# Casts, squares and folds at other steps of a fused cross-covariance attention and StarReLU kernel

## The chip, the cores and the metric

The kernel runs on one core of a Trainium2 chip. A core has a matrix engine (TensorE, in the profile PE, with its weight loads as PEld), a vector engine (VectorE, DVE), an activation engine (ScalarE, ACT), a general engine (GpSimd, POOL), and SyncE (SP), which here only issues DMAs. Each engine works through its own queue of instructions, and they wait for each other by semaphores. The metric is the device time of one execution in microseconds, lower is better; 718.1 us is the median of five runs before the change (718.03 to 718.57).

## The reference

Two layers are chained. The first is a cross-covariance attention over channels, for 4 batches of 6080 rows and 256 channels:

```python
qn = q / (np.linalg.norm(q, axis=1, keepdims=True) + 1e-06)
kn = k / (np.linalg.norm(k, axis=1, keepdims=True) + 1e-06)
s = kn.transpose(0, 2, 1) @ qn / tau
a = softmax(s)                       # over the last axis
x = (v @ a).reshape(24320, 256)
```

The second is a feed-forward layer with 2048 hidden units:

```python
h = x @ w_in
r = np.maximum(h, 0.0)
g = s * (r * r) + b                  # s and b are single numbers
out = g @ w_out
```

## The kernel before, in words

**Folding.** The attention matrix `a` of a batch (256 x 256) is multiplied into `w_in` once (`wa`, 256 x 2048), so that the hidden layer is `h = v @ wa`. The constant `b` enters as one row, `rowconst`, added at the end, and `s` as a factor of the evacuation.

**Groups and steps.** The 24320 rows of v are cut into groups of 512. A group has 16 steps, one for each 128 hidden units (`m`). The main loop runs over `s = 16 g + m`, and in each step `mm1` issues two 512-column matmuls into half of a PSUM tile `h_ps`; there are two such tiles. After every odd step ScalarE's `relu` turns one full `h_ps` tile into fp16 `r`, and so frees it: the tile written in steps 20 and 21 is written again in step 24, which can't start before the relu issued in step 21 has ended. Squares of `r` give `g`: for groups other than the first and the last, the table `SQUARES` says that two of them run on ScalarE (after steps 3 and 5 of the group) and the larger ones on VectorE (after 8 and 12, and after step 0 of the next group).

**The second matmul.** It runs one group late. For most groups the product of `g` with `w_out` is done with seven instead of eight half-size products (`seven_items`), each of 16 small matmuls, issued seven in a step from the fourth step on. They need combined weights (`T1`, `T2`, `T3`, `N4`, made from the pieces of `w_out` by `combine_w` and `cast_w`) and sums of quarters of `g` (`S1` to `S4`, by `sums_of`, VectorE). Three PSUM areas X, Y, Z are used in turn by the seven products X, Z, X, Y, X, Z, X; Z and Y lie in one tile. After each product VectorE evacuates it (`evacuate`: `u` for three of them, `o_sb` for four), and the next product in the same tile waits for that. The first group uses the plain product instead (`plain_mm2`) and needs `w_out` in fp16, piece by piece (`cast_w_out`, four pieces).

**The next batch beside it.** While the groups of batch b - 1 run, the gram matrix and the norms of batch b are made from chunks of 512 rows of k and q (`Gram`). For each chunk `norm_ops` gives up to five operations: the square of k (ScalarE), the square of q (VectorE), a first fold of both (1024 elements), a second fold (512 elements), and an accumulating DMA on GpSimd's queue (`into_first`).

**What sets the order.** Everything on the side is put at a step by hand with `at_step(s, f)`: after the matmuls of step s the functions of that step issue their instructions, in the order in which they were put there, and `po` keeps the program order on each engine. The tuples `CO`, `RC`, `CW`, `CT` hold the steps of the work on `w_out`. For the chunks of a batch, `sc` is the (fractional) step of chunk c; its loads go to `sc - 16`, its gram matmuls from `sc` on, and its norm operations to `int(sc) + 3`, and 3, 6, 9 and 12 steps later. For batch 1 (groups 0 to 10) `sc` is 26 + 6.75 c, for batch 2 it is 182 + 9.75 c, for batch 3 it is 374 + 9.75 c. The raw chunks and the fp32 pieces of `w_out` share one pool of eight buffers (`qk_pool`), so the last reader of a piece decides when a later chunk can be loaded. The squares of the chunks have two buffers (`sq_pool`).

Of the kernel before, what the change touches and what calls it, by code (L numbers as in the profile page):

```python
# [17 lines left out]
def kernel(  # L18
# [15 lines left out]
    B, N, C = q.shape  # L34
# [14 lines left out]
    NG = (NT + TG - 1) // TG  # L49
# [6 lines left out]
    def po(ins):  # L56

        tc.keep_in_program_order(ins)
        return ins
# [29 lines left out]
    T1, T2, T3, N4 = (wpool.tile([P, NP, P], FP16, name=n) for n in ("T1", "T2", "T3", "N4"))  # L89
# [287 lines left out]
    def group(g):  # L377
        t0 = g * TG
        return t0, min(TG, NT - t0) // P
# [3 lines left out]
    def load_v(g):  # L383
        t0, nj = group(g)
        v16 = vpool.tile([P, TG // P, C], FP16, tag="v16", name="v16")
        po(nc.gpsimd.dma_start(  # L386
            out=v16[:, :nj, :],
            in_=v_flat[t0 : t0 + nj * P, :].rearrange("(p j) c -> p j c", j=nj)))
        v_tiles[g] = v16

    def transpose_v(g):
        _, nj = group(g)
        v16 = v_tiles.pop(g)
        vT_ps = ps_o.tile([P, CH, TG], FP16, tag="o_ps", name="vT_ps")
        for j in range(nj):
            for ch in range(CH):
                po(nc.tensor.transpose(vT_ps[:, ch, ts(j, P)], v16[:, j, ts(ch, P)], ident16))
        vT = vtpool.tile([P, CH, TG], FP16, tag="vT", name="vT")
        po(nc.vector.tensor_copy(out=vT[:, :, : nj * P], in_=vT_ps[:, :, : nj * P]))
        vT_tiles[g] = vT  # L400

    def crossbar_v(g):

        _, nj = group(g)
        v16 = v_tiles.pop(g)
        vT = vtpool.tile([P, CH, TG], FP16, tag="vT", name="vT")
        for j in range(nj):
            po(nc.sync.dma_start_transpose(out=vT[:, :, ts(j, P)], in_=v16[:, j, :]))
        vT_tiles[g] = vT
# [126 lines left out]
    def combine_w(i, k):  # L536

        for n in (2 * k, 2 * k + 1):
            for p in (2 * i, 2 * i + 1):
                w = w_pieces[p].rearrange("p (i h) c -> p h i c", h=2)  # L540
                B11, B12 = w[:, 0, :, :P], w[:, 0, :, P:]
                B21, B22 = w[:, 1, :, :P], w[:, 1, :, P:]
                part = ts(p, 2)
                if n == 0:
                    po(nc.vector.tensor_sub(T1[:, part, :], B12, B11))
                elif n == 1:
                    po(nc.vector.tensor_sub(B12, B22, B12))
                elif n == 2:
                    po(nc.vector.tensor_add(B11, B11, B12))
                else:  # L550
                    po(nc.vector.tensor_sub(N4[:, part, :], B21, B11))

    def cast_w_out(i):
        if i == 0:
            po(nc.vector.tensor_copy(out=w_out16[:, ts(i, 4), :], in_=w_pieces[i]))
        else:
            po(nc.scalar.copy(out=w_out16[:, ts(i, 4), :], in_=w_pieces[i]))

    def cast_w(T, i):
        w = w_pieces[i].rearrange("p (i h) c -> p h i c", h=2)  # L560
        po(nc.scalar.copy(out=T[:, ts(i, 2), :], in_=w[:, 0, :, :P] if T is T2 else w[:, 0, :, P:]))
# [4 lines left out]
    def at_step(s, f):  # L566
        side.setdefault(int(s), []).append(f)
# [8 lines left out]
        out=s_out, in0=s_bc, scalar1=1.0 / (LAM * LAM))))  # L576

    RC = (13, 16, 19, 21, 23)
    CO = (7, 14, 18, 24)
    CW = (17, 20, 25, 27)  # L580
    CT = (32, 34, 36, 38)
    for i in range(NPIECE):
        at_step(CO[i], lambda i=i: cast_w_out(i))
    for i in range(NPIECE + 1):
        at_step(RC[i], lambda i=i: rowconst_sum(i))
    at_step(30, rowconst_mm)
    for i in range(NPIECE):
        at_step(CW[i], lambda i=i: combine_w(i // 2, i % 2))
        at_step(CT[i], lambda i=i: cast_w(T2, i))
        at_step(CT[i] + 6, lambda i=i: cast_w(T3, i))  # L590
    for g in range(NG):
        if g >= 3:
            at_step(max(g - 4, 0) * FT + 2, lambda g=g: load_v(g))
        if g >= 1:
            if g == 1:
                at_step(12, lambda g=g: transpose_v(g))
            else:
                at_step((g - 2) * FT + 6, lambda g=g: crossbar_v(g))
    for b in range(1, B):
        gr = grams[b]  # L600
        w0 = first_group[b - 1] * FT + (26 if b == 1 else 6)
        w1 = first_group[b] * FT - 3
        NCH = len(gr.chunks)
        fin_len = 54
        span = (w1 - fin_len) - w0 - 12
        n = NCH * JC
        for c in range(NCH):
            sc = w0 + span * c * JC / n
            at_step(max(3, sc - 16), lambda gr=gr, c=c: gr.load(c))
            if c == 0:  # L610
                at_step(sc, gr.start)
            for j in range(JC):
                at_step(w0 + span * (c * JC + j) / n, lambda gr=gr, c=c, j=j: gr.mm(c, j))

            def norm_step(gr=gr, c=c, sc=sc):
                ops = gr.norm_ops(c)
                for i, f in enumerate(ops):
                    at_step(int(sc) + 2 + 1 + i * 3, f)
            at_step(sc + 1, norm_step)

        def fin_step(gr=gr, s=w1 - fin_len):
            ops = gr.finish_ops()
            for i, f in enumerate(ops):
                at_step(int(s) + 1 + (FIN[i] if i < len(FIN) else FIN[-1] + 3 * (i - len(FIN) + 1)), f)
        at_step(w1 - fin_len - 12, fin_step)
# [15 lines left out]
    def mm1(g, m):  # L641

        _, nj = group(g)
        n = nj * P
        vT = vT_tiles[g]
        i, fh = divmod(m, 2)
        if fh == 0:
            h_tiles[g, i] = h_tile("h_ps")
        h_ps = h_tiles[g, i][:, fh, :]
        for b, p0, p1 in segments(g):  # L650
            wa = grams[b].wa
            for ci in range(CH):
                if p1 - p0 == P:
                    dst, src = h_ps[:, :n], vT[:, ci, :n]
                else:
                    dst = h_ps[:, :n].rearrange("f (j p) -> f j p", p=P)[:, :, p0:p1]
                    src = vT[:, ci, :n].rearrange("f (j p) -> f j p", p=P)[:, :, p0:p1]
                po(nc.tensor.matmul(dst, wa[:, ci, ts(m, P)], src,  # L658
                                    start=(ci == 0), stop=(ci == CH - 1), skip_group_check=True))
        if m == FT - 1:  # L660
            del vT_tiles[g]
# [9 lines left out]
    def square(g, i0, i1, engine):  # L671

        n = group(g)[1] * P
        if i0 == 0:
            g_tiles[g] = gpool.tile([P, 2, NP, TG], FP16, tag="g16", name="g16")
        src = r_tiles[g, i0 // 2][:, :, i0 % 2 : i0 % 2 + i1 - i0, :n]
        dst = g_tiles[g][:, :, i0:i1, :n]
        if engine is nc.scalar:
            po(nc.scalar.activation(out=dst, in_=src, func=AF.Square))  # L679
        else:  # L680
            po(nc.vector.tensor_mul(dst, src, src))  # L681
# [79 lines left out]
    def seven_items(g):  # L761
# [56 lines left out]
        for n, (name, a, w, after) in enumerate(products):  # L818
            for i in range(NP):
# [15 lines left out]
    plain = {0, NG - 1}  # L835
    PLAG = {0: 11, NG - 1: 5}

    SQUARES = {3: (0, 1, nc.scalar), 5: (1, 2, nc.scalar), 8: (2, 4, nc.vector),
               12: (4, 6, nc.vector)}
# [10 lines left out]
    for s in range(NS + FT):  # L850
        g, m = divmod(s, FT)
        if g < NG:
            mm1(g, m)
        for f in early.pop(s, []):
            f()

        if m == SHIFT and 0 < g and g - 1 not in plain:
            items = seven_items(g - 1)
            work.append((items, 8 if g == NG - 1 else 7))
        if work:  # L860
            items, n = work[0]
            for f in items[:n]:
                f()
            del items[:n]
            if not items:
                work.pop(0)
        for gp in plain:
            for mp in range(FT):
                if s == gp * FT + PLAG[gp] + (mp * 4 // 3 if gp == 0 else mp):
                    plain_mm2(gp, mp)  # L870
        if g < NG and m % 2 == 1:
            relu(g, m // 2)
            if g in plain:
                late = g > 0 and m // 2 % 2 == 0
                square(g, m // 2, m // 2 + 1, nc.scalar if late else nc.vector)
        if g < NG and g not in plain and m in SQUARES:
            square(g, *SQUARES[m])
        if g == NG - 1 and m in LAST:
            LAST[m]()
        elif m == 0 and 0 < g and g - 1 not in plain:  # L880
            square(g - 1, 6, 8, nc.vector)
        elif 0 < g and g - 1 not in plain and m in SUMS:
            sums_of(g - 1, SUMS[m])
        for f in side.pop(s, []):
            f()
# [34 lines left out]
```

## Time and profile before

| What | Value |
|---|---|
| median of five runs | 718.1 us |
| the profiled execution | 718.4 us, its span from first to last instruction 716.6 us |
| mean granted TensorE clock | 0.998 |
| TensorE matmul busy | 697.4 us, 97% of the span |
| VectorE busy | 624.2 us, 87% |
| ScalarE busy | 544.7 us, 76% |
| GpSimd busy | 110.8 us, 15% |
| relu on ScalarE (L668) | 384 instructions, 1014 ns mean |
| squares of `r` on VectorE (L681) | 150 instructions, 1165 ns mean |
| squares of `r` on ScalarE (L679) | 97 instructions, 1035 ns mean |

Times are counted from the first instruction of the span. Step 0 starts at 37.4 us, step 16 at 49.8, step 32 at 63.7, step 48 at 78.7. In a row of the timeline the first number is the start, the second the duration, and "xN" says that N equal instructions follow each other in it; "[idle before <-releaser]" names what ended a longer idle time. Since an engine begins its next instruction a little before the last one's end, the time that an instruction takes on its queue is read from one start to the next.

### The profile page before, as it was taken

How to read it: one execution, taken by the hardware profiler on the slowest of the kernel's cores; microseconds unless marked ns; L12 is line 12 of the kernel's file. 1: busy time of each engine (PE TensorE's matmuls, PEld its weight loads, DVE VectorE, ACT ScalarE, POOL GpSimd, SP SyncE). 2: the span in 40 equal slices, each digit the busy share in tenths (PEclk: the TensorE clock that was granted, in tenths of full speed). 3: DMA queues.
4: the chain of work that ended last, by engine and by line, in shares of the span. 5: the costliest groups of instructions: out<-in, count | busy, mean ns of one | idle time of the engine just before them, and what ended most of it. 6: DMA issues, size and time to landing. Idle time of an engine off the chain costs nothing.

```text
span 716.6 us, 17491 instructions
## 1 busy us (share of the span) xinstructions
PE 697.4 (97%) x7421; PEld 503.6 (70%) x7421; DVE 624.2 (87%) x877; ACT 544.7 (76%) x592; POOL 110.8 (15%) x189
## 2 busy tenths in 40 slices
PE   4699999999999999999999999999999999999998
PEld 2456777776677777777677777777668777777777
DVE  4889999988789989998889899998887888888886
ACT  5779877787777777778777778777877777777874
POOL 4532323202101222111010222110000000000000
PEclk9999999999999999999999999999999999999999
DMA  9999999636565978444661887853323333321201
GB/s 234 207 258 172 154 155 159 122 91 124 110 125 109 136 134 144 112 89 93 136 149 53 148 133 126 152 91 75 100 63 75 94 71 75 97 60 46 82 31 75
DMA packets 87454, 83.47 MB, mean 116 GB/s; under 512 B 56304, under 2 KB 62256, under 8 KB 87376
## 3 DMA queue, kind: packets, MB, share of 16 engines
q0 software_dynamic: 26608, 43.40, 38.6%
q1 hardware_dynamic: 60192, 37.64, 21.7%
q8 instruction: 58, 0.95, 0.6%
q10 hardware_dynamic: 576, 1.31, 0.5%
q14 instruction: 20, 0.16, 0.1%
HBM read 78.91 MB, written 24.90 MB: 145 GB/s over the span
## 4 chain that ended last, share of the span: by engine, by line
PE 93%; DMA 3%; DVE 2%; ACT 2%; issue 0%; ACTq 0%; DVEq 0%
PE h_ps L658 45%; PE o_ps L826 40%; PE s_ps L148 4%; PE wa_ps L327 2%; DMA qk<-in_k_dram 1%; DMA raw<-in_q_dram 1%; ACT sq L177 1%; PE o_ps L730 1%; DVE f L191 1%; PE o_ps L704 0%; ACT r L668 0%; ACT r L269 0%; DVE sq L174 0%; PE n_ps L244 0%; DVE o_sb L686 0%
## 5 line engine op out<-in xcount | busy, mean ns | idle before, releaser
L668 ACT ACTIVATE r<-h_ps 128x1024 f16<-128x1024 f32 (+1 forms) x384 | 388.4, 1014 | 151.8 <-PE h_ps L658 148.1
L658 PE MATMUL h_ps<-vT,wa 128*128 128x512 f16 (+7 forms) x1632 | 452.5, 365 | 0.6 <-ACT wa L320 0.5
L826 PEld LDWEIGHTS <-S 128*128 128x128 f16 x2944 | 198.0, 98 | 84.8 <-issue 0.2
L826 PEld LDWEIGHTS <-g 128*128 128x128 f16 x2208 | 155.0, 98 | 74.1
L681 DVE TENSOR_TENSOR g<-r 128x2048 f16<-128x2048 f16 (+2 forms) x150 | 174.8, 1165 | 13.9 <-ACT r L668 13.4
L826 PE MATMUL o_ps<-T,S 128*128 128x128 f16 x2208 | 183.4, 219 | 0.1
L658 PEld LDWEIGHTS <-wa 128*128 128x128 f16 x1632 | 135.9, 98 | 20.6 <-ACT wa L320 0.8
L826 PE MATMUL o_ps<-w_out,g 128*128 128x128 f16 x1472 | 134.3, 219 | 0.2 <-DVE u L686 0.2
L686 DVE SCALAR_TENSOR_TENSOR o_sb<-o_ps,s_out,u 128x256 f32<-128x256 f32 x138 | 66.5, 482 | 50.8 <-PE o_ps L826 48.9
L679 ACT ACTIVATE g<-r 128x1024 f16<-128x1024 f16 (+1 forms) x97 | 100.4, 1035 | 0.2
L148 PE MATMUL s_ps<-qk 128*128 128x256 f16 (+1 forms) x384 | 72.2, 291 | 13.6 <-ACT qk L139 9.3
L386 POOL DMA_DIRECT2D v<-in_v_dram x48 | 31.0, 648 | 263.3 <-DMA vT<-v 196.3
L686 DVE SCALAR_TENSOR_TENSOR u<-o_ps,s_out,rowconst 128x256 f32<-128x256 f32 x138 | 65.9, 478 | 0.0
L826 PE MATMUL o_ps<-w_out,S 128*128 128x128 f16 x736 | 63.5, 219 | 0.0
L826 PE MATMUL o_ps<-N,g 128*128 128x128 f16 x736 | 63.4, 219 | 0.0
L207 POOL DMA_DIRECT2D f<-f x30 | 26.3, 876 | 224.9 <-DVE f L191 180.6
L755 DVE TENSOR_TENSOR S<-S,g 128x2048 f16<-128x2048 f16 (+1 forms) x47 | 56.4, 1201 | 1.3
L177 ACT ACTIVATE sq<-qk 128x1024 f16<-128x1024 f16 (+2 forms) x53 | 54.5, 1041 | 3.9 <-DMA qk<-in_k_dram 2.6
L753 DVE TENSOR_TENSOR S<-g 128x2048 f16<-128x2048 f16 (+1 forms) x47 | 56.1, 1193 | 0.0
L759 DVE TENSOR_TENSOR S<-g,S 128x2048 f16<-128x2048 f16 x46 | 55.9, 1216 | 0.0
L757 DVE TENSOR_TENSOR S<-g 128x2048 f16<-128x2048 f16 x46 | 55.9, 1216 | 0.0
L148 PEld LDWEIGHTS <-qk 128*128 128x128 f16 (+1 forms) x384 | 33.0, 103 | 20.8 <-ACT qk L139 9.8
(83 smaller groups left out, 314.0 us busy)
## 6 DMA issues: line engine op xcount, KB each, us to landing
out_dram<-o_sb SPq DMA_DIRECT2D x42, 512.0 KB, 3.0
v<-in_v_dram POOLq DMA_DIRECT2D x47, 256.0 KB, 4.8
qk<-in_k_dram POOLq DMA_DIRECT2D x42, 256.0 KB, 6.7
qk<-in_q_dram POOLq DMA_DIRECT2D x42, 256.0 KB, 7.7
f<-f POOLq DMA_DIRECT2D x30, 128.0 KB, 3.3
vT<-v SPq DMA_TRANSPOSE x182, 3.0
out_dram<-o_sb SPq DMA_DIRECT2D x10, 256.0 KB, 4.8
w<-in_moe_w_out_dram POOLq DMA_DIRECT2D x4, 512.0 KB, 9.8
```

Of the source, the lines that this page charges most:

```text
L148: po(nc.tensor.matmul(self.s_ps[:, ch, :], qc[:np_, j, ts(ch, P)], kc[:np_, j, :], start=(c == 0 and j == 0 and ch == 0), stop=(c == len(s ...
L177: po(nc.scalar.activation(out=st["sq"][:np_, a, js, :], in_=(qc, kc)[a][:np_, js, :], func=AF.Square))
L658: po(nc.tensor.matmul(dst, wa[:, ci, ts(m, P)], src, start=(ci == 0), stop=(ci == CH - 1), skip_group_check=True))
L668: po(nc.scalar.activation(out=r16[:, :, i % 2, :n], in_=h_tiles.pop((g, i))[:, :, :n], func=AF.Relu))
L679: po(nc.scalar.activation(out=dst, in_=src, func=AF.Square))
L681: po(nc.vector.tensor_mul(dst, src, src))
L686: po(nc.vector.scalar_tensor_tensor(out=dst, in0=src, scalar=s_out, op0=ALU.mult, in1=add, op1=ALU.add))
L753: po(nc.vector.tensor_add(T[1], A21, A22))
L755: po(nc.vector.tensor_sub(T[2], T[1], A11))
L757: po(nc.vector.tensor_sub(T[3], A11, A21))
L759: po(nc.vector.tensor_sub(T[4], A12, T[2]))
L826: po(nc.tensor.matmul(st[name][:, j, :], a()[:, i, ts(j, P)], w[:, i, :], start=first, stop=last, skip_group_check=True))
```

## The change

It moves instructions to other steps; none is added or taken away.

- `w_out`'s casts to fp16 (pieces 1 to 3) go to steps 12, 14 and 18, from 14, 18 and 24. The casts of `T2` go to 28, 28, 31, 32, from 32, 34, 36, 38, and those of `T3` to 34, 36, 38, 40, from 38, 40, 42, 44.
- In group 1 the two ScalarE squares go to steps 5 and 7 of the group, from 3 and 5.
- A table `LATER` shifts single norm operations (0: square of k, 1: square of q, 2 and 3: folds, 4: the accumulating DMA) of chunks 0, 1, 2 and 11 of batch 1, and of chunks 4 and 6 of batches 2 and 3, by that many steps. The operations are put in place three steps ahead of the chunk instead of one after it, so that a negative shift is possible.

```diff
-    CO = (7, 14, 18, 24)
+    CO = (7, 12, 14, 18)
     CW = (17, 20, 25, 27)
-    CT = (32, 34, 36, 38)
+    CT = (28, 28, 31, 32)
+    CT3 = (34, 36, 38, 40)
...
         at_step(CT[i], lambda i=i: cast_w(T2, i))
-        at_step(CT[i] + 6, lambda i=i: cast_w(T3, i))
+        at_step(CT3[i], lambda i=i: cast_w(T3, i))
...
+    LATER = {(1, 0): {2: 3, 3: 1}, (1, 1): {0: 6, 1: 3, 2: 3, 3: 3, 4: 3},
+             (1, 2): {0: 4, 2: 1, 3: 1, 4: 1}, (1, 11): {2: 1, 3: 1}}
+    for b in range(2, B):
+        LATER.update({(b, 4): {2: 1}, (b, 6): {0: -2}})
...
                 ops = gr.norm_ops(c)
+                later = LATER.get((gr.b, c), {})
                 for i, f in enumerate(ops):
-                    at_step(int(sc) + 2 + 1 + i * 3, f)
-            at_step(sc + 1, norm_step)
+                    at_step(int(sc) + 3 + i * 3 + later.get(i, 0), f)
+            at_step(sc - 3, norm_step)
...
-        if g < NG and g not in plain and m in SQUARES:
-            square(g, *SQUARES[m])
+        squares = {**SQUARES, 3: (), 5: SQUARES[3], 7: SQUARES[5]} if g == 1 else SQUARES
+        if g < NG and g not in plain and squares.get(m):
+            square(g, *squares[m])
```

## The prediction

> **What bounds the kernel now.** I began with the page's engine totals and then the busy time of each engine in stretches (columns: stretch, its length, then busy us and number of instructions for TensorE matmul, weight load, VectorE, ScalarE, GpSimd; granted clock, DMA share, GB/s).
>
> ```profile
> PE 697.4 (97%) x7421; PEld 503.6 (70%) x7421; DVE 624.2 (87%) x877; ACT 544.7 (76%) x592; POOL 110.8 (15%) x189
> ...
> 43.00:76.00 33.00, 32.64 (x250) 21.09 (x248) 31.02 (x51) 30.17 (x37) 7.96 (x15) 1.00 1.10 187
> 76.00:136.00 60.00, 60.00 (x643) 44.16 (x642) 57.57 (x85) 47.62 (x51) 17.02 (x26) 1.00 1.11 156
> 242.00:265.00 23.00, 22.99 (x246) 16.68 (x245) 21.36 (x31) 17.96 (x19) 4.46 (x7) 1.00 0.99 158
> ```
>
> TensorE's busy share says it never stops after 76 us, but its spans are modelled and overlap. So I read its timeline by start times instead: a 512-column matmul is followed after 0.216 us, a 256-column one after 0.109, a 128-column one after 0.056. What exceeds these is lost. From 43 us on, the losses over 0.06 us are few. Four places, each a row and the next:
>
> ```profile
> 55.45 0.60 PE L730 MATMUL o_ps<-w_out,g 128*128 128x256 f16 x4
> 56.10 0.59 PE L658 MATMUL h_ps<-vT,wa 128*128 128x512 f16 x2
> ...
> 69.61 0.80 PE L826 MATMUL o_ps<-T,S 128*128 128x128 f16 x7
> 70.25 0.38 PE L148 MATMUL s_ps<-qk 128*128 128x256 f16 x2
> ...
> 71.72 0.61 PE L826 MATMUL o_ps<-T,S 128*128 128x128 f16 x6
> 72.55 0.22 PE L826 MATMUL o_ps<-w_out,g 128*128 128x128 f16 x1 [0.21 <-DVE u L686]
> ...
> 262.50 0.22 PE L826 MATMUL o_ps<-w_out,g 128*128 128x128 f16 x1
> 262.73 0.59 PE L658 MATMUL h_ps<-vT,wa 128*128 128x512 f16 x2
> ```
>
> Row by row: 4 x 0.109 after 55.45 is 55.89, the next starts at 56.10 (0.22 lost); 7 x 0.056 after 69.61 is 70.00, next 70.25 (0.25); 6 x 0.056 after 71.72 is 72.06, next 72.55 (0.12 + 0.38); 262.56 against 262.73 (0.18). The whole list: 0.04 at 50.0; 0.22, 0.12 and 0.13 at 55.8, 57.7 and 59.6; 0.25, 0.12, 0.38 and 0.05 at 69.8, 71.8, 72.1 and 72.7; 0.07 at 139.5; 0.12 and 0.18 at 247.6 and 262.5; the same two at 420.3 and 435.2; and, away from the change, 0.17 at 43.1 and 0.14 at 703.5. TensorE is the bound, and **1.96 us** is all that lies in the change's reach.
>
> Who is late shows in the other queues at those times. ScalarE ahead of 56.10:
>
> ```profile
> 54.08 1.06 ACT L679 ACTIVATE g<-r 128x1024 f16<-128x1024 f16 x1
> 55.03 1.02 ACT L668 ACTIVATE r<-h_ps 128x1024 f16<-128x1024 f32 x1
> 55.93 1.07 ACT L679 ACTIVATE g<-r 128x1024 f16<-128x1024 f16 x1
> 56.88 1.03 ACT L668 ACTIVATE r<-h_ps 128x1024 f16<-128x1024 f32 x1
> 57.78 1.06 ACT L557 CAST w_out<-w 128x1024 f16<-128x1024 f32 x1
> ```
>
> The relu at 55.03 (its input ready at 54.31) frees the `h_ps` buffer that step 24 writes; it ends at 56.05, and step 24 starts at 56.10. Squares (L679) and a cast (L557) stand ahead of three relus in turn. VectorE ahead of 70.04 and 72.55:
>
> ```profile
> 68.95 0.69 DVE L191 TENSOR_TENSOR f<-sq 128x1024 f16<-128x1024 f16 x1
> 69.55 0.48 DVE L686 SCALAR_TENSOR_TENSOR u<-o_ps,s_out,rowconst 128x256 f32<-128x256 f32 x1
> 69.95 1.22 DVE L757 TENSOR_TENSOR S<-g 128x2048 f16<-128x2048 f16 x1
> 71.08 0.42 DVE L191 TENSOR_TENSOR f<-f 128x512 f16<-128x512 f16 x1
> 71.42 0.69 DVE L174 TENSOR_TENSOR sq<-qk 128x1024 f16<-128x1024 f16 x1
> 72.02 0.48 DVE L686 SCALAR_TENSOR_TENSOR u<-o_ps,s_out,rowconst 128x256 f32<-128x256 f32 x1
> ```
>
> Each evacuation `u` ends where the third and the fourth product can start (70.03, 72.50); folds and a square of the next batch stand just ahead of it.
>
> **What the Trainium skill says.** "TensorE: Matmul & The Clock Gate", section "Wait — 56ns, not 53.3ns?", gives back-to-back warm matmuls as 55.6 and 215.7 ns for 128 and 512 columns; the trace's 56 and 216 agree, so the sums above measure loss. The same page, on engine queue depths, has ScalarE and VectorE as strict FIFO: what is moved ahead delays all behind it, as the rows above show. "Perfetto Trace Analysis", section "Identifying the Most-Contended Engine", calls matmul busy share a bad measure; here 60.00 of 60 agrees. "VectorE: DVE Perf Modes", section "The perf-mode tier table", has a 2048-element 16-bit tensor_tensor at 1224 ns; the trace has 1.22.
>
> **The change part by part.** No instruction is added or removed; TensorE's and SyncE's orders stay as they are. On one queue an instruction costs its start-to-start time: relu 0.92, ScalarE square or large cast 0.95, small cast 0.30; VectorE 2048-element ops 1.13, square or first fold 0.60, second fold 0.34, evacuation 0.40.
>
> *Casts and squares, steps 7 to 31.* The casts of pieces 1 to 3 move to steps 12, 14, 18. Step 12's fills idle ScalarE time: free at 47.03, done at 48.07, next relu at 48.24. Its data landed at 45.16. It also ends the 0.04 at 50.0. The others take the slots of the earlier two; their data landed at 46.67 and 48.07, before 49.16 and 52.23. Group 1's squares move from steps 19 and 21 to 21 and 23. So the relu of step 21 starts at 54.31 and ends at 55.33; square; relu of step 23 at 56.18 to 57.21; square; relu of step 25 waits for that square's end (58.16; it reuses the tile) and runs 58.19 to 59.24. TensorE asks for these at 55.84, 57.58 and 59.31 (56.10, 57.96 and 59.82 less the losses up to there). All are in time, the last by 0.02 after a release of 0.05. Gain 0.04 + 0.47. The T2 casts at 28 and 31 come after their inputs (the last combine for them ends at 61.2) and end by 64.4; the 0.12 at 71.8, a wait for T2's last piece, goes. T3's last cast ends near 71.4 instead of 76.5; its product starts later.
>
> *Folds and squares of batch 1, chunks 0 to 2.* VectorE is one unbroken queue here. It starts group 1's square (57.94, waiting for a relu) at 57.77. Adding start-to-start times, with the own-result waits seen before, S1 starts at 66.28, S2 at 67.54, then `u` at once: 68.67 to 69.15, where TensorE asks at 69.33 (69.84 less 0.51; later ones likewise). Then S3 (69.07), fold (70.20), second `u` 70.80 to 71.28, asked at 71.29. On to the evacuation of the fifth product at 77.55 to 78.02, asked at 78.09, now behind a fold and a square of chunks 1 and 2. The relu freeing step 42's buffer, now without two squares and casts ahead of it, ends at 71.13, asked at 71.6. The pinch: between 57.77 and 82 VectorE idled 0.17 (before 57.94), 0.44 (72.42 to 72.86) and 0.60 (78.99 to 79.59), 1.21 in all, and the same work stands in it after the change. So it can come out **1.21** earlier, not the 1.30 that TensorE's list (0.04 + 0.47 + 0.79) offers; 0.09 returns as a wait for the next `u`, near 84.6.
>
> *Chunk 11 of batch 1.* A fold (0.60) goes behind an evacuation: the 0.07 at 139.5 goes. *Batches 2 and 3, chunk 4.* The fold goes behind the second `u`: 0.12 each. *Chunk 6.* A ScalarE square moves from behind step 243's square into step 241, where ScalarE idled 0.84 ahead of step 243's relu; 0.95 of work delays that relu some 0.05, and the relu that TensorE waits for at 262.7 comes about 0.9 earlier: 0.18 each. Together 0.07 + 0.59. Its data landed at 238.3, 18 us ahead.
>
> *GpSimd.* One accumulating DMA moves from step 47 to 50, behind a load of v and of chunk 6; it no longer holds them (they were issued at 78.99 behind its 78.38). Buffers freed earlier by T3 let chunk 4's load go at about 66 instead of 67.3. Nothing on TensorE waited for a DMA after 43 us. I take nothing; chunk 2 still lands about 3 us ahead of its use.
>
> Sum: 1.21 + 0.07 + 0.59 = 1.87. The three slacks below 0.1 may leak; I take 0.02 for it. The profiled execution took 718.4 (span 716.6, 1.8 around it), 0.3 over the median of 718.1; the change alters only the span, to 714.75. From the median: **716.25**.
>
> **The rivals.** A measurement of this kernel tells 0.2%, 1.44 us, from no change.
>
> *The slacks fail.* The relu of step 25, the second `u` and the fifth evacuation have 0.02, 0 and 0.07 in hand. If each is late by 0.2, the first part keeps 0.6 to 0.7: 716.8 (down to 717.3 if later batches also give half). For: VectorE has no idle left. Against: every duration is measured and the order of work fixed.
>
> *No effect.* The stalls are as long elsewhere, or the engines' waits just move by one instruction: 718. For: VectorE 57.57 of 60 after 76 us. Against: the list of idle times above.
>
> *Slower.* The fold of chunk 1 at step 44 stands ahead of the square of step 44 and the fifth evacuation, and waits for a ScalarE square that stands behind step 41's relu. If that ended after 76.3 the whole VectorE queue would stop, and TensorE with it, one for one. It should end at 73.3; to eat 1.87 and cost 1.44 more it must come 6.3 late: 719.6. Against: no ScalarE backlog over 1 us exists there.
>
> **How the numbers follow.** As forecast 0.73 (716.0 to 716.6); slacks fail 0.17; no effect 0.07; slower 0.03. The first is faster by over 0.2%, with a fifth of the second: 0.76; within 0.2%: 0.20; slower: 0.04. The range 715.8 to 717.2 holds the first and most of the second; its low end is all 1.96 and a little scatter.
>
> **What would show it.** No L658 row of TensorE more than 0.1 late at 55 to 60; the relu of step 21 near 54.3; `u` before the first fold, near 68.7; VectorE unbroken from 57.8 to 80; step 50's S1 near 80.9; no loss at about 247 and 262. Wrong if a new loss over 0.2 stands at steps 28, 41 or 48, or if ScalarE's relus there wait for something other than TensorE.

## The result, and the profile after

| | before | after |
|---|---|---|
| median | 718.26 us (717.99 to 718.75, 43 runs) | 716.60 us (716.35 to 717.01, 25 runs) |
| ratio | | 0.9977, 95% interval 0.9972 to 0.9983 |
| profiled execution | 718.4 us, span 716.6 | 717.0 us, span 715.2 |

The change takes 1.66 us (0.23%) off. The forecast was 716.25 with 715.8 to 717.2 around it. The measured time lies in the range, 0.35 above the middle: 0.16 of this is the kernel before, which came out at 718.26 beside the changed one instead of 718.1, and 0.19 is gain that was forecast (1.85) and did not come.

The engine totals and the same stretches of the changed kernel (columns as for the kernel before; 76 to 242 us is left out):

```profile
PE 694.6 (97%) x7421; PEld 502.8 (70%) x7421; DVE 624.0 (87%) x877; ACT 545.0 (76%) x592; POOL 110.9 (16%) x189
...
43.00:76.00 33.00, 32.87 (x259) 21.67 (x257) 31.46 (x52) 30.49 (x38) 9.54 (x18) 1.00 1.06 201
...
242.00:265.00 23.00, 23.00 (x250) 16.85 (x249) 22.23 (x32) 17.68 (x19) 4.46 (x7) 1.00 0.96 158
```

In the same 33 us TensorE now issues 259 matmuls instead of 250, and VectorE and ScalarE are busier. Of the totals only TensorE's two change by more than 0.3 us (matmuls by 2.8, weight loads by 0.8). Its timeline at the places that were shown before:

```profile
55.63 0.60 PE L736 MATMUL o_ps<-w_out,g 128*128 128x256 f16 x4
56.06 0.59 PE L664 MATMUL h_ps<-vT,wa 128*128 128x512 f16 x2
...
67.47 0.28 PE L832 MATMUL o_ps<-w_out,g 128*128 128x128 f16 x2
67.87 0.45 PE L832 MATMUL o_ps<-T,S 128*128 128x128 f16 x5
...
69.64 0.55 PE L832 MATMUL o_ps<-T,S 128*128 128x128 f16 x7
70.03 0.38 PE L148 MATMUL s_ps<-qk 128*128 128x256 f16 x2
...
71.50 0.50 PE L832 MATMUL o_ps<-T,S 128*128 128x128 f16 x6
71.83 0.22 PE L832 MATMUL o_ps<-w_out,g 128*128 128x128 f16 x1
...
261.54 0.22 PE L832 MATMUL o_ps<-w_out,g 128*128 128x128 f16 x1
261.60 0.60 PE L664 MATMUL h_ps<-vT,wa 128*128 128x512 f16 x2
```

55.63 + 4 x 0.109 is 56.07: nothing lost where 0.22 were. 69.64 + 7 x 0.056 is 70.03, and 71.50 + 6 x 0.056 is 71.84: the 0.25 and the 0.50 are gone. 261.54 + 0.056 is 261.60: the 0.18 is gone. But 67.47 + 2 x 0.056 is 67.58, and the second product starts at 67.87: **a new loss of 0.29 us**, where the kernel before lost nothing. All losses over 0.03 us from 43 us on are now this one and the two away from the change (0.17 at 43.3, 0.14 at 702.1). Two fp32 matmuls of `rowconst` near 62 us take 0.107 more than an fp16 one of their size in every trace, before and after; they are not counted as losses. So 1.96 of losses went and 0.29 came: 1.67 us, against 1.66 between the medians. The profiled execution's span shrank by only 1.4 because its first 43 us, which the change does not touch, took 0.22 longer (that first loss stands at 43.30 instead of 43.08); times below are from executions whose heads differ by up to 0.5.

The relus of steps 21, 23 and 25 on ScalarE answer to those at 55.03, 56.88 and 58.72 before:

```profile
54.53 1.02 ACT L674 ACTIVATE r<-h_ps 128x1024 f16<-128x1024 f32 x1 [0.15 <-PE h_ps L664]
...
56.39 1.02 ACT L674 ACTIVATE r<-h_ps 128x1024 f16<-128x1024 f32 x1
57.30 1.06 ACT L685 ACTIVATE g<-r 128x1024 f16<-128x1024 f16 x1
58.38 1.94 ACT L674 ACTIVATE r<-h_ps 128x1024 f16<-128x1024 f32 x2
```

Less the head's 0.22 they start at 54.31, 56.17 and 58.16; the forecast had 54.31, 56.18 and 58.19. The third is the one that waits for the square ahead of it to end. VectorE around the new loss:

```profile
66.00 0.69 DVE L174 TENSOR_TENSOR sq<-qk 128x1024 f16<-128x1024 f16 x1
66.60 1.22 DVE L759 TENSOR_TENSOR S<-g 128x2048 f16<-128x2048 f16 x1
67.85 1.23 DVE L761 TENSOR_TENSOR S<-S,g 128x2048 f16<-128x2048 f16 x1
68.99 0.48 DVE L692 SCALAR_TENSOR_TENSOR u<-o_ps,s_out,rowconst 128x256 f32<-128x256 f32 x1
...
71.12 0.48 DVE L692 SCALAR_TENSOR_TENSOR u<-o_ps,s_out,rowconst 128x256 f32<-128x256 f32 x1
...
78.83 0.48 DVE L692 SCALAR_TENSOR_TENSOR o_sb<-o_ps,s_out,u 128x256 f32<-128x256 f32 x1 [0.18 <-PE o_ps L832]
```

S1 (66.60; the second row) ends at 67.82, and the second product, which multiplies S1 by T1, starts 0.05 later. The first `u` stands right behind S2 and ends at 69.47, 0.4 ahead of the third product, which is the fifth matmul of the row at 69.64. The second `u` ends at 71.60, 0.23 ahead of the fourth product at 71.83. At 78.83 VectorE waits for TensorE: it has been free since about 78.58.

### The profile page after: what moved, and what is told of

Same layout as the page of the kernel before. It is cut to its first block, busy times and chain, and to the rows that moved or that the text cites. A ratio compares the mean times of both kernels' runs of the same rounds, so it can differ in the third digit from the quotient of the medians.

```text
span 715.2 us, 17493 instructions
## 1 busy us (share of the span) xinstructions
PE 694.6 (97%) x7421; PEld 502.8 (70%) x7421; DVE 624.0 (87%) x877; ACT 545.0 (76%) x592; POOL 110.9 (16%) x189
## 4 chain that ended last, share of the span: by engine, by line
PE 92%; DVE 3%; DMA 3%; ACT 2%; issue 0%; DVEq 0%; ACTq 0%
PE h_ps L664 45%; PE o_ps L832 40%; PE s_ps L148 4%; PE wa_ps L327 2%; DMA qk<-in_k_dram 1%; DMA raw<-in_q_dram 1%; ACT sq L177 1%; DVE g L687 1%; PE o_ps L710 0%; DVE acc L526 0%; DVE f L191 0%; ACT r L269 0%; PE n_ps L244 0%; DVE w L547 0%; DVE o_sb L692 0%
```

## The experiments

Each was run beside the kernel before on the same chip; "before" is that kernel's median there, 718.18 to 718.39. "Loss" means TensorE's start-to-start time over 0.216, 0.109 or 0.056 us (512, 256 or 128 columns, fp16) in the run's own trace.

**The parts alone.** First the casts and group 1's squares, with the table of shifts empty:

```diff
-    LATER = {(1, 0): {2: 3, 3: 1}, (1, 1): {0: 6, 1: 3, 2: 3, 3: 3, 4: 3},
-             (1, 2): {0: 4, 2: 1, 3: 1, 4: 1}, (1, 11): {2: 1, 3: 1}}
-    for b in range(2, B):
-        LATER.update({(b, 4): {2: 1}, (b, 6): {0: -2}})
+    LATER = {}
```

> The casts and group 1's squares moved as in the change; no fold or square of a chunk moved. The list of TensorE's losses alone (each loss goes with its own cause) says 0.04 + 0.47 + 0.12 = 0.63 us less than before, 717.6. My theory, VectorE as the bound from 57.8 us on: TensorE comes 0.5 us earlier to the first S1 and finds it not ready (a new loss of about 0.3 where the second product starts, as in the changed kernel), and the u behind the fold is late by another 0.25 and 0.5; only the 0.17 us that VectorE idled before 57.94 and the 0.05 at 72.7 are gained: 0.22 us, 718.0, no difference that can be measured. The losses at 55.8, 57.7 and 59.6 are gone in both; the losses near 70 and 72 tell the two apart.

Measured: 718.25 us (13 runs) against 718.28; ratio 0.9999 (0.9991 to 1.0007). The trace decides where the times can't. TensorE's timeline:

```profile
67.30 0.28 PE L829 MATMUL o_ps<-w_out,g 128*128 128x128 f16 x2
67.71 0.45 PE L829 MATMUL o_ps<-T,S 128*128 128x128 f16 x5
...
71.59 0.50 PE L829 MATMUL o_ps<-T,S 128*128 128x128 f16 x6
72.42 0.22 PE L829 MATMUL o_ps<-w_out,g 128*128 128x128 f16 x1 [0.33 <-DVE u L689]
```

The losses up to 59.6 are gone, and 0.29, 0.26 and 0.49 stand at 67.4, 69.6 and 71.9, in place of 0.25, 0.12, 0.38 and 0.05. So of 0.63 us of ScalarE's waits removed, 0.25 stays as a gain by the trace (1.30 of losses before 73 us, 1.05 now) and nothing can be measured: TensorE runs ahead and meets VectorE. The list of losses is not a sum of independent gains. The 0.29 at the second product stands here too, though no fold or square of a chunk was moved.

Then batch 1's shifts alone, with the old casts and squares:

```diff
-    CO = (7, 12, 14, 18)
+    CO = (7, 14, 18, 24)
-    CT = (28, 28, 31, 32)
-    CT3 = (34, 36, 38, 40)
+    CT = (32, 34, 36, 38)
+    CT3 = (38, 40, 42, 44)
...
-             (1, 2): {0: 4, 2: 1, 3: 1, 4: 1}, (1, 11): {2: 1, 3: 1}}
-    for b in range(2, B):
-        LATER.update({(b, 4): {2: 1}, (b, 6): {0: -2}})
+             (1, 2): {0: 4, 2: 1, 3: 1, 4: 1}}
...
-        squares = {**SQUARES, 3: (), 5: SQUARES[3], 7: SQUARES[5]} if g == 1 else SQUARES
+        squares = SQUARES
```

> The shifts of chunks 0, 1 and 2 of batch 1 alone; casts, group 1's squares and later batches as before. Both theories: the losses of 0.04, 0.22, 0.12 and 0.13 up to 59.6 stay; those at 69.8, 71.8, 72.1 and 72.7 go (0.79 us, 717.5). S1 is ready at 67.78 as before and TensorE asks for it at 67.86, so there is no loss at the start of the second product. A loss there would say that the moved folds, not the earlier TensorE, make S1 late.

Measured: 717.80 us, but over 717.30 to 719.74 in 21 runs, ratio 0.9995 (0.9988 to 1.0002). The four losses near 70 to 73 are gone and none stands at the second product, as expected. With the run before, this says that it is the earlier TensorE, not the moved folds, that finds S1 not ready. What nobody expected is a loss of 0.42 at a gram matmul:

```profile
114.58 0.55 PE L830 MATMUL o_ps<-T,S 128*128 128x128 f16 x7
115.39 0.39 PE L148 MATMUL s_ps<-qk 128*128 128x256 f16 x2 [0.25 <-DMA qk<-in_q_dram]
```

Chunk 9's load landed at 115.3; TensorE asked for it at 115.0 and used it at 115.4. In the changed kernel it landed at 105.4 for 114.8, in the kernel before at 111.7 for 115.6. GpSimd's queue, which issues the loads, shows where the time went:

```profile
79.21 0.89 POOL L207 DMA_DIRECT2D f<-f  x1 [5.43 <-DVE f L191]
90.08 0.87 POOL L207 DMA_DIRECT2D f<-f  x1 [9.98 <-DMA f<-f]
```

The accumulating DMA of chunk 1 was issued at 79.21 and landed at 89.5, 1.0 us after chunk 6's load, issued before it, had landed at 88.5. The next one must wait for that landing, and every load stands behind it. The spread of the times fits such a DMA that lands now earlier, now later. Which part of the change keeps this away in the changed kernel is asked below.

The later batches alone (chunk 11 of batch 1, chunks 4 and 6 of batches 2 and 3; casts, squares and chunks 0 to 2 as before):

```diff
-    LATER = {(1, 0): {2: 3, 3: 1}, (1, 1): {0: 6, 1: 3, 2: 3, 3: 3, 4: 3},
-             (1, 2): {0: 4, 2: 1, 3: 1, 4: 1}, (1, 11): {2: 1, 3: 1}}
+    LATER = {(1, 11): {2: 1, 3: 1}}
     for b in range(2, B):
         LATER.update({(b, 4): {2: 1}, (b, 6): {0: -2}})
```

> The shifts of chunk 11 of batch 1 and of chunks 4 and 6 of batches 2 and 3 alone. The 0.07 at 139.5, and 0.12 and 0.18 in each of batches 2 and 3 go, the losses up to 73 us stay: 0.66 us, 717.6. If these waits only move on by one instruction, losses of the same size stand within 10 us behind them and the time is as before, 718.26.

Measured: 717.75 us (717.39 to 718.03, 21 runs), 0.53 less than before; ratio 0.9992 (0.9986 to 0.9999). In the trace all five losses (0.66) are gone and nothing new stands behind them: these waits were taken away, not moved on.

**The new loss.** The changed kernel with VectorE's square of chunk 0 behind S1, and a fold of chunk 0 and a square of chunk 2 moved behind an evacuation (a second fold of chunk 0 goes one step later):

```diff
-    LATER = {(1, 0): {2: 3, 3: 1}, (1, 1): {0: 6, 1: 3, 2: 3, 3: 3, 4: 3},
-             (1, 2): {0: 4, 2: 1, 3: 1, 4: 1}, (1, 11): {2: 1, 3: 1}}
+    LATER = {(1, 0): {1: 2, 2: 4, 3: 2}, (1, 1): {0: 6, 1: 3, 2: 3, 3: 3, 4: 3},
+             (1, 2): {0: 4, 1: 1, 2: 1, 3: 1, 4: 1}, (1, 11): {2: 1, 3: 1}}
```

> The changed kernel, with VectorE's square of chunk 0 put behind S1 (two steps later), its first fold behind the second u, its second fold one step later, and VectorE's square of chunk 2 behind the evacuation of the fifth product. If the new loss of 0.29 us at the start of the second product is VectorE's square ahead of S1: S1 starts 0.48 us earlier, the loss is gone, no other comes, and the time is 0.2 to 0.3 us under the changed kernel, about 716.35. If VectorE's whole queue between 57.8 and 82 is the bound (1.21 us in all), 0.1 of it comes back as a wait of TensorE before step 55. If the second product waits for something else (a cast, a weight), the loss stays at 0.29.

Measured: 716.31 us (716.16 to 716.73, 6 runs), ratio 0.9972 (0.9961 to 0.9984), 0.29 under the changed kernel's median. VectorE's and TensorE's timelines:

```profile
64.51 1.22 DVE L687 TENSOR_TENSOR g<-r 128x2048 f16<-128x2048 f16 x1
65.75 1.23 DVE L759 TENSOR_TENSOR S<-g 128x2048 f16<-128x2048 f16 x1
```

```profile
67.11 0.28 PE L832 MATMUL o_ps<-w_out,g 128*128 128x128 f16 x2
67.23 0.44 PE L832 MATMUL o_ps<-T,S 128*128 128x128 f16 x5
```

S1 now follows its own input at once and ends at 66.98; the second product starts 0.12 after 67.11, with no loss. One of 0.05 stands at 84.5, on the `u` where the forecast saw 0.09 coming back. So the order of work ahead of S1 made the loss; this run moves four operations, and the next one the square alone.

The opposite: VectorE's square of chunk 0 issued twice in the changed kernel.

```diff
-                        po(nc.vector.tensor_mul(
+                        for _ in range(2 if (self.b, c) == (1, 0) else 1):
+                          po(nc.vector.tensor_mul(
                             st["sq"][:np_, 0, js, :], qc[:np_, js, :], qc[:np_, js, :]))
```

> The changed kernel with VectorE's square of chunk 0 of batch 1 issued twice (0.60 us of work that changes no result, just ahead of S1). If S1 is late because VectorE's queue is full, S1 comes 0.60 later, the loss at the start of the second product grows from 0.29 to 0.89, nothing of it is made up, and the time is 0.60 over the changed kernel: 717.2. If VectorE has room there (the 0.25 us idle before 78.8), at most 0.35 remains. If S1 isn't what is waited for, nothing changes.

Measured: 717.29 us (717.16 to 717.77, 21 runs), 0.69 over the changed kernel's median; ratio to before 0.9986 (0.9979 to 0.9993). TensorE:

```profile
66.98 0.28 PE L833 MATMUL o_ps<-w_out,g 128*128 128x128 f16 x2
68.11 0.45 PE L833 MATMUL o_ps<-T,S 128*128 128x128 f16 x5 [0.85 <-DVE S L760]
```

The loss is 1.02, or 0.72 more. The second square did not take 0.60: it writes the tile that the first one wrote, waits for its end, and starts 0.72 after it. VectorE's queue has no room there: what is put ahead of S1 is paid in full, and no later idle time makes up for it.

**The loads.** The changed kernel with T2's and T3's casts at their old steps:

```diff
-    CT = (28, 28, 31, 32)
-    CT3 = (34, 36, 38, 40)
+    CT = (32, 34, 36, 38)
+    CT3 = (38, 40, 42, 44)
```

> The changed kernel with the casts of T2 and T3 back at their old steps (32, 34, 36, 38 and 38, 40, 42, 44); all else as changed. By ScalarE's queue alone nothing is lost: T2's last piece is cast by 70.7, TensorE needs it at about 71.7; 716.6. By the buffers: T3's casts are the last readers of the four pieces of w_out, whose buffers the chunks 5 to 8 then wait for, so the loads of chunks 6 to 9 go out later and land later, as in the run with batch 1's shifts alone (chunk 9 landed at 115.3 for a use at 115.4); a gram matmul (L148) waits near 90 to 116 for up to 1.5 us in some executions, and the times spread by more than 1 us: median 716.7 to 717.6.

Measured: 716.54 us (9 runs), ratio 0.9977 (0.9967 to 0.9987): the median is what ScalarE's queue alone said, and not the 716.7 to 717.6 of the buffers. But two of the nine took 717.44 and 717.58, and the profiled one of these has a loss of 0.49 at a gram matmul, as the buffers said: TensorE asked for chunk 9 at 114.7, and it landed at 115.2. On the path that ScalarE and VectorE set, the T casts' new steps bring nothing; for the loads they bring 9 us of slack.

Batch 1's shifts alone, twice more: once with the accumulating DMA of chunk 1 left at step 47, ahead of step 50's loads, and once with the new steps of the T casts.

```diff
-    LATER = {(1, 0): {2: 3, 3: 1}, (1, 1): {0: 6, 1: 3, 2: 3, 3: 3, 4: 3},
+    LATER = {(1, 0): {2: 3, 3: 1}, (1, 1): {0: 6, 1: 3, 2: 3, 3: 3},
```

> Batch 1's shifts alone, with the accumulating DMA of chunk 1 left at step 47, ahead of the loads of step 50, instead of at step 50 behind them. If its place behind the loads is what held up GpSimd's queue (it landed at 89.5, and the next accumulating DMA waits for its landing), it lands near 83, chunk 7's load goes out near 86 instead of 90.6, chunk 9 lands 3 us or more before its use, the 0.42 us at 114.9 are gone, and the times lie within 0.7 us of each other near 717.5. If not, chunk 9 still lands within 1 us of its use and the spread of 2.4 us stays.

Measured: 717.47 us (717.25 to 717.84, 21 runs), ratio 0.9989 (0.9982 to 0.9995). The DMA, issued at 79.3, landed at 83.1, chunk 7's load went out at 85.2 and chunk 9 landed at 110.2 for a use at 115.0.

```diff
-    CT = (32, 34, 36, 38)
-    CT3 = (38, 40, 42, 44)
+    CT = (28, 28, 31, 32)
+    CT3 = (34, 36, 38, 40)
```

> Batch 1's shifts together with the changed steps of T2's and T3's casts; w_out's casts, group 1's squares and later batches as before. If early T3 casts are what keeps the loads early, chunk 6's load goes out near 69 instead of 72.7, chunk 9 lands near 105 for a use at 115, no gram matmul waits, and the times are within 0.7 us of each other at 717.5. If the casts do nothing, the loss near 115 and the spread stay as without them.

Measured: 717.43 us (717.26 to 717.87, 21 runs), ratio 0.9987 (0.9980 to 0.9994). Chunk 6's load went out at 69.0 (72.7 without the early casts), chunk 9 landed at 106.0 for a use at 114.5. Either remedy removes the loss and the spread (2.4 us without, 0.6 with). So two parts of the change belong together: moving the accumulating DMA behind the loads puts GpSimd's queue at the mercy of how late those loads are, and the earlier T3 casts, which free the buffers of `w_out`'s pieces, make them early enough. That the late landing is what spreads the times is shown in part: of the slower executions one has a trace (717.44, with the T casts at their old steps), and the wait for the late load is 0.49 of its 0.90 over the median. The slowest, up to 719.74, have none.

**The same kernel again, and a better one.** The changed kernel was run once more beside a version that keeps the reordering with S1 first and moves half of S2 in the last group:

> The changed kernel once more, beside the next run on the same chip: 716.6, with one loss of 0.29 us at the start of the second product of the first seven-product group and 0.14 near 702, and gram matmuls never waiting for a load.

Measured: 716.66 us (716.42 to 717.01, 11 runs), the losses of 0.29 and 0.14 as expected.

```diff
-    LAST = {0: last_squares, 2: lambda: sums_of(NG - 2, 1, NP // 2, NP),
-            3: lambda: sums_of(NG - 2, 2, 0, NP // 2), 5: lambda: sums_of(NG - 2, 2, NP // 2, NP)}
+    LAST = {0: last_squares, 2: lambda: (sums_of(NG - 2, 1, NP // 2, NP), sums_of(NG - 2, 2, 0, NP // 2)),
+            3: lambda: None, 5: lambda: sums_of(NG - 2, 2, NP // 2, NP)}
```

> The reordering of the run with S1 ahead of the square, and one more: in the last group the first half of S2 is issued at step 754, right behind the second half of S1, instead of at 755 behind a square of the last group. The 0.29 is gone as there; near 702 VectorE's u comes 0.2 to 0.3 earlier and the 0.14 goes too: about 0.4 us under the changed kernel, 716.2. If the wait near 702 is set by the end of the first product instead of VectorE's queue, it stays and the time is 716.3.

Measured: 716.11 us (716.00 to 716.31, 6 runs), ratio to before 0.9969 (0.9957 to 0.9981), 0.55 under the changed kernel beside it. Both losses are gone; from 42 us on, TensorE loses 0.17 at 42.8 (where it waits for a block of `wa`) and 0.05 at 84.3. This is the fastest version run.

## Why the prediction was right

**What bounds the kernel.** Right: TensorE's start-to-start losses were what this change could gain. Before 1.96, after 0.29, difference 1.67; measured 1.66. That the two agree to 0.01 is luck: in the other runs, but for the two in which a load was late, the losses that went and the difference of the medians lie 0.02 to 0.22 apart. One reading beside it was wrong: the 60.00 of 60 us busy does not show that the busy share misleads, since nothing was lost there. The 22.99 of 23.00 from 242 to 265 us does, with 0.30 lost in them.

**Casts and squares, steps 7 to 31.** Right, within 0.03 us for each of the three relus, and the 0.02 in hand at step 28 held. The T casts' 0.12 was credited here; the run with old T casts shows that with the other shifts in place it would have gone without them.

**Folds and squares of batch 1: the step that was mis-sized.** That VectorE is one unbroken queue here was right, and so were the order and the durations. Two things were wrong. First, the working compared VectorE with what TensorE asks only from the third product on. In the kernel before, S1 had ended at 67.78 and the second product had started at 67.86: no loss, hence not in the list, but a slack of under 0.1. TensorE, 0.51 earlier than before, now asks for it at 67.36 (67.58 less the head's 0.22). Second, the sum up to S1 is 0.1 short. From group 1's square to S1 the order of work does not change, and it takes 8.61 us in both traces; the forecast's 57.77 and 66.28 leave 8.51. Only the first of the three idle times, 0.17, lies ahead of S1, so S1 could not come more than 0.17 earlier than 66.56. It started at 66.38 and ended at 67.60, which is the 0.24 after 67.36 that, with 0.05 for the release, makes the 0.29.

So the term of 1.21 for steps 7 to 50 measured 1.01 (1.30 of losses gone, 0.29 come). VectorE's S1 of step 50 is 0.98 earlier than before, not 1.21: since TensorE had lost the 0.29, it was late at 78.8, and VectorE idled 0.25 there that was forecast as filled. The 1.21 itself was nearly right as a bound: with S1 put first, the losses up to 90 us fall by 1.25 in all, and the 0.05 that comes back stands at the `u` that was named.

**Chunk 11, later batches.** Right, each to 0.01 in the trace: 0.66 gone, none back, and alone they give 0.53 of it in the times.

**GpSimd.** "I take nothing" held for the changed kernel, where gram matmuls never wait. The reason given was too short: that no load was late before said nothing of loads behind a moved accumulating DMA. It holds because the T casts moved too. The runs moved those of T2 and T3 together; that T3's are the ones that count is read from the code, where they read the pieces of `w_out` last.

**The rivals.** "The slacks fail" named the second `u`, the fifth evacuation and the relu of step 25. The relu held. The other two held by luck, because TensorE was already 0.29 late: the second `u` ended at 71.60 for a product at 71.83, which without the delay would have been asked for at 71.54; the fifth evacuation ended at 78.32 for a product at 78.63, or 78.34 without the delay, which leaves less than the 0.05 that a release takes. What failed by 0.29 is a slack that was not on the list, S1. The signs of being wrong named a new loss over 0.2 at steps 28, 41 or 48; one of that size came at step 37, which the prediction did not watch. So the time lies where the forecast had it, at the upper end of 716.0 to 716.6, with a small form of this rival in it. "No effect" and "slower" fall with the trace: no fold waited for a late ScalarE square.

## What to carry to other kernels

A list of an engine's losses is an upper bound on what removing them gives: before adding them up, ask of every other result that the engine uses how early it is, those that are just in time above all, since they show as no wait at all. When the casts' waits alone were removed here, 0.63 us of them turned into 0.25 by the trace and nothing that could be measured. And when an instruction on a queue of DMAs waits for another DMA's landing, its place among the loads matters even while nothing waits for the loads yet.

## What was not expected

- Two VectorE instructions that write the same tile one after the other start 0.72 us apart, where independent ones of the same size start 0.60 apart.
- An accumulating DMA of 128 KB (that of chunk 1) landed 3.9 us after issue when it stood ahead of a group of loads on GpSimd's queue and 10.3 us after when it stood behind them (batch 1's shifts alone). Behind them it landed 0.8 to 2.7 us after the last of them in four traces, and so only 6.5 us after issue in the changed kernel, where these loads went out earlier.
- The head of the kernel varies: the same loss at step 8 stands anywhere from 42.8 to 43.3 us in the twelve profiled executions.
